# The first four chunks of q and k loaded in float32 by another queue, and the constants behind them

## The chip, the cores and the metric

The kernel runs on one core of a Trainium2 chip. A core has five engines with their own instruction streams: TensorE (PE in the profile, with its weight loads as PEld), VectorE (DVE), ScalarE (ACT), GpSimd (POOL) and SyncE (SP). Transfers between the chip's large memory and the core's on-chip memory run on 16 DMA engines that all queues share. Each engine that issues transfers has a queue of its own: GpSimd's is q0 in the profile, SyncE's q1, ScalarE's q10. The metric is the device time of one execution in microseconds.

## The reference

```python
qn = q / (np.linalg.norm(q, axis=1, keepdims=True) + 1e-06)
kn = k / (np.linalg.norm(k, axis=1, keepdims=True) + 1e-06)
s = kn.transpose(0, 2, 1) @ qn / tau
s = s - s.max(-1, keepdims=True)
a = np.exp(s)
a /= a.sum(-1, keepdims=True) + 1e-09
x = (v @ a).reshape(B * N, C)
logits = x @ w_gate
# softmax weights w of the two largest logits of each row, 0 elsewhere
out = x + sum over experts e of w[:, e] * ((x @ A[e]) @ B[e])
```

There are 4 batches of 6400 rows and 256 columns in float32. Within a batch, q and k give a 256x256 matrix (the Gram matrix of the columns, scaled by the column norms), its softmax `a` multiplies v, and each row of the result then goes through a mixture of 8 small adapters of rank 16. Read are 78.6 MB of q, k and v and 0.27 MB of constants; written are 26.2 MB.

## The kernel before

A batch's 6400 rows are split over the 128 partitions, 50 rows to a partition. One such set of 128 rows is a chunk, and 10 chunks are a tile: 640 KB of bfloat16 for each of q, k and v. Loads go through GpSimd's queue, which converts float32 to bfloat16 on the way. For the four batches there are 20 tiles of q and k together (four buffers) and 20 of v (five buffers).

The list `loads` (L89 to L97) fixes the order of all loads: first batch 0's five tiles of q and k (numbered 0 to 4 in this text), then batch 1's q and k mixed with batch 0's v, and so on. `load_more` (L107) issues the next entries of the list until a buffer is still in use by work not yet written into the program. GpSimd then waits for the release of the buffer and for one of eight DMA lanes, so that at most eight of its loads are under way. Tiles 0 to 3 fill the four buffers at once. Tile 4 (loaded in two parts, of 6 and 4 chunks) needs tile 0's buffer, batch 1's first tile needs tile 1's, and everything after it in the list stands behind it on GpSimd.

The program's order is written out by hand, instruction by instruction. At its start SyncE loads the three constants (L137 to L139): w_gate (8 KB, `wst`), moe_A (128 KB, `ast`, read in pieces of 128 bytes, 1024 of them) and moe_B (128 KB, `bst`, rows of 1 KB). GpSimd issues tiles 0 to 2 (L140), makes two identity matrices (L141 to L144) and issues tile 3 (L151). VectorE fills small constants and casts the three loaded ones to bfloat16 (L156 to L159); these casts stand ahead of all its other work and wait for the three transfers.

Then comes batch 0's loop over pairs of chunks (L479 to L486). For each pair, `square` squares q and k into one of five `sq` buffers (VectorE and ScalarE in turn), `gram` multiplies the two chunks of k by those of q on TensorE (L182), and `norm` sums the squares of the chunks four earlier by a matmul with ones (L194). When all 50 chunks are in, a chain of small steps (`chain0` to `chain6`) makes the softmax matrix and folds the cast constants into it; `ident_f` is first read in `chain1`, `ident` in `chain4`, `A_sb` and `wg_sb` in `chain5`.

After this the loop over slots mixes the work on batch 0's v (transposes L316, gating, L422 to L458, output copies L462) with the Gram matrix of the next batch, and so on through the batches. Outputs are collected in `ys`, eight buffers of 10 chunks, and sent by ScalarE's queue, late, and at the end by SyncE's.

Of the kernel before, what the change touches and what calls it, by code (L numbers as in the profile page):

```python
# [8 lines left out]
FP32 = mybir.dt.float32  # L9
BF16 = mybir.dt.bfloat16  # L10
# [6 lines left out]
def kernel(  # L17
# [16 lines left out]
    nc = tc.nc  # L34
    B, N, C = q.shape
    P = 128
    NC = N // P
    CC = C // P
    E = moe_w_gate.shape[1]
    R = moe_A.shape[2]  # L40
# [4 lines left out]
    PC = 10  # L45
    NPAIR = NC // 2
    NPT = B * NPAIR
    GRP = 5
    QKB, VB, YB = 4, 5, 8
    DEFER = 6  # L50

    GRAM = {1: (0, 20), 2: (24, 45), 3: (49, 67)}
# [2 lines left out]
    q_v = q.rearrange("b (p c) d -> b p c d", p=P)  # L55
    k_v = k.rearrange("b (p c) d -> b p c d", p=P)
# [3 lines left out]
    const = ctx.enter_context(tc.tile_pool(name="const", bufs=1))  # L60
# [4 lines left out]
    y_pool = ctx.enter_context(tc.tile_pool(name="yp", bufs=YB))  # L65
# [15 lines left out]
    for b, (first, last) in GRAM.items():  # L81
        n = last - first + 1
        for c in range(NC):
            s = first + c * n // NC
# [3 lines left out]

    loads = []  # L89
    for s in range(NC // PC):  # L90
        loads.append((-10 + s, "qk", 0, s, [PC] if s < NC // PC - 1 else [6, 4]))
        for b in range(1, B):
            loads.append((qk_need[b, s], "qk", b, s, [PC]))
        for b in range(B):
            loads.append((NPAIR * b + s * PC // 2 + 1, "v", b, s,
                          [6, 4] if b == B - 1 and s == NC // PC - 1 else [PC]))
    loads.sort(key=lambda x: x[0])  # L97
    tiles = {"qk": {}, "v": {}}
# [8 lines left out]
    def load_more(limit=1000):  # L107

        while limit and at_load[0] < len(loads):
            _, kind, b, s, parts = loads[at_load[0]]  # L110
            n = len(left[kind])
            if n >= bufs[kind] and left[kind][n - bufs[kind]]:
                return
            where[kind, b, s] = n
            left[kind].append(PC)
            c0 = s * PC
            if kind == "qk":
                t = qk_pool.tile([P, 2, PC, C], BF16, tag="qk", name="qk")
            else:
                t = v_pool.tile([P, PC, C], BF16, tag="v", name="vt")  # L120
            tiles[kind][b, s] = t
            o = 0
            for m in parts:
                if kind == "qk":
                    nc.gpsimd.dma_start(t[:, 0, o:o + m, :], q_v[b, :, c0 + o:c0 + o + m, :])  # L125
                    nc.gpsimd.dma_start(t[:, 1, o:o + m, :], k_v[b, :, c0 + o:c0 + o + m, :])
                else:
                    nc.gpsimd.dma_start(t[:, o:o + m, :], v_v[b, :, c0 + o:c0 + o + m, :])  # L128
                o += m
            at_load[0] += 1  # L130
            limit -= 1


    wst = const.tile([P, CC * E], FP32)
    ast = const.tile([P, E, CC * R], FP32)
    bst = const.tile([P, C], FP32)
    nc.sync.dma_start(wst, moe_w_gate.rearrange("(p cc) e -> p (cc e)", p=P))  # L137
    nc.sync.dma_start(ast, moe_A.rearrange("e (p cc) r -> p e (cc r)", p=P))
    nc.sync.dma_start(bst, moe_B.rearrange("e r d -> (e r) d"))  # L139
    load_more(3)  # L140
    ident = const.tile([P, P], BF16)  # L141
    make_identity(nc, ident)
    ident_f = const.tile([P, P], FP32)
    make_identity(nc, ident_f)  # L144
    ones_bf = const.tile([P, 2], BF16)
    nc.vector.memset(ones_bf, 1.0)
    ones_f = const.tile([P, P], FP32)
    nc.vector.memset(ones_f, 1.0)
    neg_inv_tau = const.tile([P, 1], FP32)
    nc.vector.memset(neg_inv_tau, -inv_tau)  # L150
    load_more(3)  # L151

    wg_sb = const.tile([P, CC, E], BF16)
    A_sb = const.tile([P, CC, E, R], BF16)
    ball_sb = const.tile([P, C], BF16)
    nc.vector.tensor_copy(wg_sb.rearrange("p cc e -> p (cc e)"), wst)  # L156
    for cc in range(CC):
        nc.vector.tensor_copy(A_sb[:, cc, :, :], ast[:, :, cc * R:(cc + 1) * R])
    nc.vector.tensor_copy(ball_sb, bst)  # L159


    acc, nrm, sqs = {}, {}, {}
# [1 line left out]
    def square(b, c, eng):  # L164

        s, o = divmod(c, PC)
        t = tiles["qk"][b, s]
        sq = sq_pool.tile([P, 2, 2, C], BF16, tag="sq", name="sq")
        sqs[b, c] = sq
        src = t[:, :, o:o + 2, :]  # L170
        if eng == "act":
            nc.scalar.activation(sq, src, ACT.Square)  # L172
        else:
            nc.vector.tensor_tensor(out=sq, in0=src, in1=src, op=OP.mult)  # L174

    def gram(b, c):
        if c == 0:
            acc[b] = ps_acc.tile([P, CC, C], FP32, tag="acc", name="acc")
        s, o = divmod(c, PC)
        t = tiles["qk"][b, s]  # L180
        for ic in range(CC):
            nc.tensor.matmul(  # L182
                acc[b][:, ic, :], t[:, 1, o, ic * P:(ic + 1) * P], t[:, 0, o, :],
                start=(c == 0 and ic == 0), stop=(c == NC - 1), skip_group_check=True)
        used("qk", b, c, 1)

    def norm(b, c):
        if c == 0:
            nrm[b] = ps_nrm.tile([P, 512], FP32, tag="nrm", name="nrm")
        sq = sqs[b, c - c % 2]  # L190
        for w in range(2):
            for ic in range(CC):
                j = w * CC + ic
                nc.tensor.matmul(  # L194
                    nrm[b][:, j:j + 1], sq[:, w, c % 2, ic * P:(ic + 1) * P], ones_bf[:, 0:1],
                    start=(c == 0 and j == 0), stop=(c == NC - 1), skip_group_check=True)
# [272 lines left out]
    def send(keep):  # L469


        eng = nc.scalar if keep else nc.sync
        while len(unsent) > keep:
            gr = unsent.pop(0)
            c0, n = 2 * (gr["f"] - gr["b"] * NPAIR), 2 * gr["n"]
            eng.dma_start(out_v[gr["b"], :, c0:c0 + n, :], gr["ys"][:, 0:n, :])


    for c in range(0, NC, 2):  # L479
        square(0, c, "act" if (c // 2) % 2 else "dve")  # L480
        gram(0, c)
        gram(0, c + 1)
        load_more()
        if c >= 4:
            norm(0, c - 4)
            norm(0, c - 3)  # L486
# [31 lines left out]
    while nz < NPT or zq is not None or dq is not None:  # L518
# [26 lines left out]
        dq, zq = zq, u  # L545
        send(max(0, min(DEFER, DEFER - (slot - GRAM[B - 1][1]) // 4)))
        if behind:
# [53 lines left out]
```

## Time and profile before

| | us |
|---|---|
| Median of three runs (257.8 to 257.87) | 257.8 |
| The profiled execution | 257.84 |
| Its span in the profile | 256.1 |
| Busy in the span: TensorE | 217.3 (85%) |
| ScalarE | 174.7 (68%) |
| VectorE | 150.6 (59%) |
| GpSimd | 34.5 (13%) |
| GpSimd's queue q0 (39.33 MB written), share of 16 engines | 75.7% |
| ScalarE's queue q10 (19.66 MB) | 18.6% |
| SyncE's queue q1 (6.82 MB) | 6.8% |

How to read the profile: the span is cut into 40 slices of 6.4 us, and each digit of a slice line is a busy share in tenths. The chain of waits follows the work that ended last back to its start; its lines give a start, a length and what ran. A wait is named by the engine that waited and by what released it. The queue lines give packets, megabytes and the time that the packets took as a share of 16 engines; since packets overlap, it can exceed 100%. GpSimd's queue is counted by what it writes, in bfloat16, while it reads twice as much. The times of a transfer run from its issue to its landing.

The first instructions around the change, by the timeline: SyncE issues w_gate at 0.74, moe_A at 1.18 and moe_B at 1.65 us. GpSimd issues tile 0 at 1.24 and 1.89 us, tiles 1 and 2 until 4.55 us, makes the identities between 4.49 and 5.63 us and issues tile 3 at 5.58 and 6.12 us. VectorE casts w_gate at 2.36, moe_A at 4.06 and moe_B at 10.03 us. Tile 0 lands at about 10.9 us, and TensorE's first matmul starts at 10.98 us.

### The profile page before, as it was taken

To read this page: it belongs to the slowest core of one execution; us is meant where nothing else is said; L and a number is where in the kernel's file an instruction comes from. 1 tells how busy PE (TensorE), PEld (TensorE's weight loads), DVE (VectorE), ACT (ScalarE), POOL (GpSimd) and SP (SyncE) were. 2 spreads that over 40 slices of the span, in tenths; PEclk is the share of its full clock that TensorE was granted. 3 is DMA by queue.
4 is the path that set the end of the run, shared out by engine and by line. 5 is a ranking of instruction groups with operands and counts; after the bars stand their busy time and mean duration, and the time that the engine had idled before them with its cause. 6 is when DMAs were issued, how large, how long until landed. Compare 5 with 4: busy or idle time off the path is not lost.

```text
span 256.1 us, 7681 instructions
## 1 busy us (share of the span) xinstructions
PE 217.3 (85%) x3256; PEld 192.1 (75%) x3256; DVE 150.6 (59%) x573; ACT 174.7 (68%) x288; POOL 34.5 (13%) x71
## 2 busy tenths in 40 slices
PE   0277694977898999999999999999799999999970
PEld 0256582766797978989999788988698789999960
DVE  1323234246746678676776776757477777777830
ACT  2234257366596698887977878787678768877870
POOL 8031131111112110120210203000000100000000
PEclk9987787579999999999999999999999999999997
DMA  6999999999999999999999999999999999999994
GB/s 117 222 214 214 210 215 215 214 213 215 214 215 214 215 214 216 213 215 214 213 215 215 313 281 248 246 285 300 229 281 271 325 337 366 421 418 425 425 380 181
DMA packets 13890, 66.30 MB, mean 259 GB/s; under 512 B 2592, under 2 KB 2720, under 8 KB 11424
## 3 DMA queue, kind: packets, MB, share of 16 engines
q0 software_dynamic: 9072, 39.33, 75.7%
q10 hardware_dynamic: 2160, 19.66, 18.6%
q1 hardware_dynamic: 2624, 6.82, 6.8%
q8 instruction: 25, 0.41, 0.6%
q14 instruction: 9, 0.07, 0.1%
HBM read 78.91 MB, written 26.21 MB: 411 GB/s over the span
## 4 chain that ended last, share of the span: by engine, by line
PE 44%; DMA 39%; DVE 8%; ACT 3%; issue 2%; POOL 1%; DVEq 0%; ACTq 0%; POOLq 0%
DMA qk<-in_k_dram 24%; PE y_ps L438 12%; DMA vt<-in_v_dram 8%; PE acc L182 7%; DMA qk<-in_q_dram 6%; PE zg L422 6%; PE y_ps L458 5%; PE vT_ps L316 5%; PE zg L446 3%; PE vT_ps L337 3%; PE nrm L194 2%; DVE gz L426 2%; ACT sq L172 2%; ACT ys L462 1%; DVE e L368 1%
## 5 line engine op out<-in xcount | busy, mean ns | idle before, releaser
L172 ACT ACTIVATE sq<-qk 128x1024 bf16<-128x1024 bf16 x87 | 89.0, 1053 | 36.4 <-DMA qk<-in_k_dram 35.3
L182 PE MATMUL acc<-qk 128*128 128x256 bf16 x400 | 78.3, 300 | 21.6 <-DMA qk<-in_k_dram 21.6
L462 ACT COPY ys<-y_ps 128x512 f32<-128x512 f32 x100 | 58.7, 587 | 18.0 <-PE y_ps L458 16.5
L438 PE MATMUL y_ps<-a_bf,vT 128*128 128x256 bf16 x400 | 59.9, 272 | 0.0
L182 PEld LDWEIGHTS <-qk 128*128 128x128 bf16 x400 | 33.7, 104 | 26.0 <-DMA qk<-in_k_dram 22.8
L194 PEld LDWEIGHTS <-sq 128*128 128x128 bf16 x800 | 46.2, 100 | 9.3 <-ACT sq L172 3.1
L426 DVE TENSOR_TENSOR gz<-zg,gate 128x256 bf16<-128x256 f32 x100 | 41.7, 417 | 14.6 <-PE zg L422 13.1
L194 PE MATMUL nrm<-ones_bf,sq 128*128 128x1 bf16 x800 | 44.9, 165 | 1.2 <-ACT sq L172 1.2
L327 DVE COPY vT<-vT_ps 128x512 bf16<-128x512 bf16 x63 | 26.7, 423 | 31.7 <-PE vT_ps L316 31.0
L316 PE MATMUL vT_ps<-ident,vt 128*128 128x128 bf16 x400 | 39.8, 224 | 2.0 <-DMA vt<-in_v_dram 1.8
L422 PE MATMUL zg<-wa_sb,vT 128*128 128x128 bf16 x400 | 38.3, 218 | 1.6 <-DVE gzT L452 1.4
L458 PE MATMUL y_ps<-ball_sb,gzT 128*128 128x256 bf16 x200 | 38.2, 273 | 0.0
L438 PEld LDWEIGHTS <-vT 128*128 128x128 bf16 x400 | 33.4, 97 | 2.5
L316 PEld LDWEIGHTS <-vt 128*128 128x128 bf16 x400 | 30.0, 99 | 5.4 <-DMA vt<-in_v_dram 2.9
L325 ACT COPY vT<-vT_ps 128x512 bf16<-128x512 bf16 x37 | 21.7, 586 | 10.6 <-PE vT_ps L316 9.0
L422 PEld LDWEIGHTS <-vT 128*128 128x128 bf16 x400 | 26.0, 96 | 3.8 <-issue 2.6
L446 PE MATMUL zg<-ident,gz 128*128 128x128 bf16 x200 | 27.6, 219 | 1.1 <-DVE gz L426 0.6
L452 DVE COPY gzT<-zg 128x256 bf16<-128x256 bf16 x90 | 25.3, 281 | 0.0
L125 POOL DMA_DIRECT2D qk<-in_q_dram x21 | 11.3, 540 | 83.0 <-ACT sq L172 18.6
L128 POOL DMA_DIRECT2D vt<-in_v_dram x21 | 11.1, 531 | 69.5 <-PE y_ps L458 39.2
L174 DVE TENSOR_TENSOR sq<-qk 128x1024 bf16<-128x1024 bf16 x13 | 8.7, 690 | 18.1 <-DMA qk<-in_k_dram 16.8
L446 PEld LDWEIGHTS <-gz 128*128 128x128 bf16 x200 | 15.1, 98 | 2.9 <-DVE gz L426 2.5
(54 smaller groups left out, 158.5 us busy)
## 6 DMA issues: line engine op xcount, KB each, us to landing
out_dram<-ys ACTq DMA_DIRECT2D x15, 1280.0 KB, 14.0
qk<-in_q_dram POOLq DMA_DIRECT2D x19, 640.0 KB, 22.1
qk<-in_k_dram POOLq DMA_DIRECT2D x19, 640.0 KB, 24.2
vt<-in_v_dram POOLq DMA_DIRECT2D x19, 640.0 KB, 24.5
out_dram<-ys SPq DMA_DIRECT2D x4, 1280.0 KB, 10.3
out_dram<-ys SPq DMA_DIRECT2D x5, 256.0 KB, 6.8
qk<-in_q_dram POOLq DMA_DIRECT2D x1, 384.0 KB, 16.4
qk<-in_k_dram POOLq DMA_DIRECT2D x1, 384.0 KB, 17.7
```

The lines of the kernel that those rows point to most:

```text
L172: nc.scalar.activation(sq, src, ACT.Square)
L182: nc.tensor.matmul(acc[b][:, ic, :], t[:, 1, o, ic * P:(ic + 1) * P], t[:, 0, o, :], start=(c == 0 and ic == 0), stop=(c == NC - 1), skip_ ...
L194: nc.tensor.matmul(nrm[b][:, j:j + 1], sq[:, w, c % 2, ic * P:(ic + 1) * P], ones_bf[:, 0:1], start=(c == 0 and j == 0), stop=(c == NC - 1 ...
L316: nc.tensor.matmul(pt[:, ic, sc * P:(sc + 1) * P], vt[:, o + sc, ic * P:(ic + 1) * P], ident, is_transpose=True, start=(i == 0), stop=(i = ...
L327: nc.vector.tensor_copy(dst, src)
L422: nc.tensor.matmul(z[:, sc, :], r["vT"][:, ic, sc, :], st[b]["wa"][:, ic, E:E + ER], start=(sc == 0 and ic == 0), stop=(sc == 1 and ic == ...
L426: nc.vector.tensor_tensor(out=gz.rearrange("p c (e r) -> p c e r", e=E), in0=z.rearrange("p c (e r) -> p c e r", e=E), in1=gr["gate"][:, r ...
L438: nc.tensor.matmul(y[:, sc, :], r["vT"][:, ic, sc, :], st[b]["a"][:, ic, :], start=(sc == 0 and ic == 0), stop=False, skip_group_check=True)
L446: nc.tensor.matmul(gt[:, sc, :], r["gz"][:, sc, :], ident, is_transpose=True, start=(sc == 0), stop=(sc == 1))
L452: nc.vector.tensor_copy(gzT, gt)
L458: nc.tensor.matmul(r["y"][:, sc, :], r["gzT"][:, sc, :], ball_sb, start=False, stop=(sc == 1), skip_group_check=True)
L462: nc.scalar.copy(gr["ys"][:, r["w"]:r["w"] + 2, :], r["y"])
```

## The change

Four chunks of q and four of k of batch 0 no longer go through GpSimd's queue. SyncE loads them first of all, in float32, into a buffer of the output pool (`stage`), 512 KB each. VectorE casts the four chunks of q to bfloat16 in two instructions, ScalarE those of k in two, into their places in tile 0; GpSimd's loads of tile 0 now begin at chunk 4. SyncE loads the constants behind the stage, moe_A last instead of moe_B. GpSimd issues tile 3 ahead of the two identities. The casts of the constants move into batch 0's loop, ahead of the work of chunk 14; VectorE meets them after its square of chunk 12 and ahead of its square of chunk 16.

```diff
+    FIRST = 4
...
-        loads.append((-10 + s, "qk", 0, s, [PC] if s < NC // PC - 1 else [6, 4]))
+        loads.append((-10 + s, "qk", 0, s, {0: [PC - FIRST], NC // PC - 1: [6, 4]}.get(s, [PC])))
...
+            o = PC - sum(parts)
...
-            o = 0
...
+    stage = y_pool.tile([P, 2 * GRP, C], FP32, tag="ys", name="stage")[:, 0:2 * FIRST, :].rearrange(
+        "p (w c) d -> p w c d", w=2)
+    nc.sync.dma_start(stage[:, 0, :, :], q_v[0, :, 0:FIRST, :])
+    nc.sync.dma_start(stage[:, 1, :, :], k_v[0, :, 0:FIRST, :])
...
     nc.sync.dma_start(wst, moe_w_gate.rearrange("(p cc) e -> p (cc e)", p=P))
+    nc.sync.dma_start(bst, moe_B.rearrange("e r d -> (e r) d"))
     nc.sync.dma_start(ast, moe_A.rearrange("e (p cc) r -> p e (cc r)", p=P))
-    nc.sync.dma_start(bst, moe_B.rearrange("e r d -> (e r) d"))
     load_more(3)
-    ident = const.tile([P, P], BF16)
-    make_identity(nc, ident)
-    ident_f = const.tile([P, P], FP32)
-    make_identity(nc, ident_f)
...
+    for c in range(0, FIRST, 2):
+        t = tiles["qk"][0, 0]
+        nc.vector.tensor_copy(t[:, 0, c:c + 2, :], stage[:, 0, c:c + 2, :])
+        nc.scalar.copy(t[:, 1, c:c + 2, :], stage[:, 1, c:c + 2, :])
+    load_more(1)
+    ident = const.tile([P, P], BF16)
+    make_identity(nc, ident)
+    ident_f = const.tile([P, P], FP32)
+    make_identity(nc, ident_f)
     load_more(3)
...
-    nc.vector.tensor_copy(wg_sb.rearrange("p cc e -> p (cc e)"), wst)
-    for cc in range(CC):
-        nc.vector.tensor_copy(A_sb[:, cc, :, :], ast[:, :, cc * R:(cc + 1) * R])
-    nc.vector.tensor_copy(ball_sb, bst)
+
+    def cast_constants():
+        nc.vector.tensor_copy(wg_sb.rearrange("p cc e -> p (cc e)"), wst)
+        for cc in range(CC):
+            nc.vector.tensor_copy(A_sb[:, cc, :, :], ast[:, :, cc * R:(cc + 1) * R])
+        nc.vector.tensor_copy(ball_sb, bst)
...
     for c in range(0, NC, 2):
+        if c == 14:
+            cast_constants()
         square(0, c, "act" if (c // 2) % 2 else "dve")
```

## The prediction

> **What bounds the kernel now.** I read the slices of the page first, then the chain of waits of the first 60 us, then the DMA queues in short windows.
>
> ```profile
> DMA  6999999999999999999999999999999999999994
> ```
>
> ```profile
> 0.64 0.60 issue
> 1.24 0.66 POOL qk L125
> 1.89 9.04 DMA qk<-in_k_dram
> ...
> 15.59 16.38 DMA qk<-in_q_dram
> ...
> 34.07 20.61 DMA vt<-in_v_dram
> 54.68 0.28 issue
> 54.97 24.46 DMA qk<-in_k_dram
> ```
>
> The DMA engines are full from the second slice almost to the end, and up to 79.4 us the chain is transfers. After that TensorE and the queue take turns: TensorE carries the chain from 80 to 154 us, a k load issued at 154.61 lands at 182.8, and the rest is TensorE. So the stream of transfers has no hole except at its start, and a stream that starts earlier moves all behind it. How much is lost there is told by the queues in 0 to 12 us and 12 to 24 us (packets, MB, share):
>
> ```profile
> q0 software_dynamic: 368, 1.72, 74.3%
> q1 hardware_dynamic: 1328, 0.27, 11.6%
> ```
>
> ```profile
> q0 software_dynamic: 565, 2.57, 104.8%
> ```
>
> A full GpSimd queue (q0) writes 2.57/12 = 0.214 MB/us. In the first 12 us it wrote 1.72 MB, which is 8.03 us of a full stream: 3.97 us are lost, to idleness and to the 0.27 MB of constants on SyncE's queue (q1).
>
> When each queue starts is seen in windows of 0.2 us: in 1.6 to 1.8 us
>
> ```profile
> q1 hardware_dynamic: 41, 0.00, 11.6%
> ```
>
> and the first packets of q0 only in 2.8 to 3.0 us:
>
> ```profile
> q1 hardware_dynamic: 257, 0.03, 103.3%
> q0 software_dynamic: 3, 0.02, 91.2%
> ```
>
> SyncE issued its first load at 0.74, GpSimd at 1.24 us: from issue to data 0.95 us on the one, 1.56 us on the other.
>
> **The change, part by part.**
>
> *The start.* SyncE's first issue, at 0.74 us, now carries 512 KB of q instead of 8 KB of w_gate, and k follows some 0.4 us later (its issues now take 0.38 to 0.57 us). So full traffic begins at 1.7 us, not at 2.8. The stage's 1.05 MB of float32 replace 0.52 MB of bfloat16 on q0. That is no extra work: at 0.214 MB/us the 0.52 MB cost 2.45 us, and in 222 to 234 us, where only float32 output moves, 426 GB/s make 1.05 MB cost 2.46 us. The stage keeps the engines busy until q0 starts at 2.8 us.
>
> The new loss is 1.7 us of idleness plus the constants, which no longer fall into an idle time. By bytes these cost 0.27/0.426 = 0.63 us. By q1's share of 0 to 4, 4 to 8 and 8 to 12 us (22.8%, 8.0%, 4.1% of 4 us) they cost 1.40 us. Between the two: moe_A's 1024 packets ran at 579 in 0.4 us (2.4 to 2.8 us), so 0.71 us, and the other 0.14 MB cost 0.33 us; I take 1.04. New loss 2.74 us (2.33 to 3.10), gain 3.97 - 2.74 = 1.2 us (0.9 to 1.6).
>
> The Trainium skill (DMA: Bandwidth & Descriptors, Specifications) gives a first-byte latency of about 1 us for the GpSimd path and 0.6 us for SyncE's. By it the start moves by the 0.5 us between the issues and 0.4 us of latency, 0.9 in all, an estimate that would give 256.9; the rows show 1.1, and I go by them.
>
> *The casts.* Two VectorE casts of 128x512 from float32. No row has them; the 128x256 cast (L159) took 0.29 us, the 128x512 bf16 copy 0.42 us, so 0.29 to 0.58 each; I take 0.5, 1.0 us in all. Two ScalarE copies: the 128x512 copy of L462 takes 0.59, 1.2 us in all. Both engines are idle until 11.02 us now, waiting for tile 0. The stage lands between about 5 us (ahead of q0) and 8 us (alternating with q0 row by row), the casts end by 9.5 us at the latest, and tile 0's six other chunks land at about 10.93 - 1.2 = 9.7. Cost nothing. Were this cover gone, tile 0 would be released later, which matters only if its successor's load (15.59 us) came after the queued three tiles (18 us of work) had run out.
>
> *GpSimd's order.* Tile 3's two loads come before the identities, so they are issued about 1.1 us earlier, behind a full queue: nothing gained. The identities come 1.1 us later; their first readers are at 39.46 and 41.99 us. Nothing.
>
> *Pool and lanes.* The stage takes the first of the eight output buffers, and each output still waits for the buffer and the DMA lane of eight before. Outputs first go out at 137.9 us. Nothing.
>
> *The casts of the constants.* 0.17 + 0.54 + 0.29 = 1.0 us of VectorE move from its idle start to behind its fourth square (c = 12, about 16 us). What queues behind is VectorE's square of c = 16 (at 18.26 us now), which TensorE reads (norm) only after tile 2 has landed, at 23.2 us, and which holds the release of tile 1; GpSimd issues into that buffer at 22.18 us. So up to about 21 us the cover is there, if the constants have landed. They are now issued last: this is where the change can turn (first rival).
>
> *Sum.* 257.84 us (the profiled run: span 256.1 and 1.7 around it; the median is 257.8) - 1.2 = 256.6. It is carried to the end because TensorE itself waits for transfers, 3.2 us in 36 to 62 us, 1.6 us in 62 to 90 us, and last for the k load that lands at 182.8 us; it starts earlier with them.
>
> **Rivals.**
>
> *Slower: moe_A is starved.* Where q1 and q0 both have work, they take turns packet by packet. In 5.8 to 9.0 us (moe_B's 1 KB rows against 5 KB rows) and in 142 to 147 us (10 KB output rows):
>
> ```profile
> q0 software_dynamic: 131, 0.59, 90.0%
> q1 hardware_dynamic: 125, 0.13, 13.9%
> ```
>
> ```profile
> q10 hardware_dynamic: 108, 1.11, 54.0%
> q0 software_dynamic: 105, 0.49, 47.4%
> ```
>
> moe_A is 64 packets of 128 B per engine, and a semaphore. Before, it ran at 2.2 to 3.7 us, mostly ahead of q0. Now k, w_gate, moe_B and moe_A (9 + 9 + 9 + 65 = 92 packets per engine) stand against q0, which has 9 per load: 18 of tile 0, 54 of tiles 1 to 3, then tile 4's. One for one, moe_A lands with the 20th of tile 4: 2.74 (lost) + 2.45 (stage) + 3.67 (rest of tile 0) + 3 x 6.12 (1.31 MB a tile) = 27.2 us to the end of tile 3, and 3.9 more, 31.1. VectorE stands still from 16 to 31 us with the square of c = 16 behind it. Tile 1 is released at 31.1 + 0.54 + 0.29 + 0.69 = 32.6, GpSimd's next load gives data 1.56 us later at 34.2, but the queue ran dry at 33.3 (five tiles of 6.12, and 2.74). That is 0.9 us idle, or up to 2.9 if the slowest engine counts (tile 4 lands at 36.45 us now, 2 us after its mean). TensorE also finishes batch 0 some 8 us late. Its later waits for DMA (3.2 us in 36 to 62, 1.6 in 62 to 90) and its low clock there (0.50 to 0.72 from 42 to 60 us) give back 5 to 8, so 0 to 3 us remain. In all 256.6 + 0.9 to 5.9: 257.5 to 262.5, middle 259.4. It decides when moe_A lands later than about 29.5 us. Against it: nothing in this trace shows small packets beside a full q0, and if a row's eight pieces go as one packet, the four need 36 turns, moe_A lands with the end of tile 1 near 15 us (2.74 + 2.45 + 3.67 + 6.12), and VectorE does not wait.
>
> The Trainium skill (DMA: Bandwidth & Descriptors, Queues, rings and completion order) says that an engine changes rows only after a whole packet, typically 9 to 17 descriptors. By that rule moe_A would need 4 to 7 turns and the forecast of 256.6 would hold; the two rows above show turns of one row each, so the rule does not settle it.
>
> *No change: swallowed.* TensorE's clock is granted at 0.50 to 0.94 between 12 and 60 us, in a pattern that follows its pauses. It now starts some 3 to 5 us earlier and pauses again for the rest of tile 0. TensorE is busy 28.4 us in 36 to 72 us; 4% more at a worse pattern is 1.2 us. Against it: in that stretch it waits for DMA anyway. Time 257.8.
>
> **Numbers.** Forecast 0.48 (256.2 to 256.9 by the bounds of the gain), starved moe_A 0.36, swallowed 0.12, 0.04 for a loss I don't see. A measurement of this kernel can tell 0.2%, 0.5 us. Faster: 0.48 and 0.02 of the starved case. Within 0.2%: 0.06 of the starved case, 0.09 of the swallowed one. Slower: 0.28, 0.03 and 0.04. The range goes from 256.1 (0.1 below the largest gain, about the spread of the runs) to 260.2 and leaves out the upper part of the starved case.
>
> **What would show it.** Right: first large packets on q1 at 1.7 us, q0's bytes in 0 to 12 us plus half of the stage's 1.05 MB near 1.98 MB (1.72 + 1.2 x 0.214), tile 1's first square near 15.9 us instead of 17.15, the k landing at 182.8 us about 1.2 us earlier, no long wait of VectorE for moe_A. Wrong: a VectorE wait on moe_A that ends near 30 us, a square of c = 16 behind it, GpSimd's fifth pair of q and k loads after 30 us, and a dip in the DMA row near 34 us.

## The result, and the profile after

The changed kernel takes 258.34 us (median of 13 runs), the kernel before 257.8 us in the same session: a ratio of 1.0021, 95% interval 1.0014 to 1.0029. It is 0.5 us slower, just at the edge of what can be told from no change. The forecast of 256.6 us has the wrong sign. What happened is the first rival, moe_A starved, in the lower part of its 257.5 to 262.5 us. One run of the kernel before and one with the stage of half the size took 493 us; no ratio below counts them.

The profiled execution of the changed kernel took 258.57 us with a span of 256.8. From its timeline (start, length, engine, line, what; in brackets the idle time before and what ended it):

```profile
16.82 0.17 DVE L169 CAST wg_sb<-wst 128x16 bf16<-128x16 f32 x1
...
32.07 0.36 DVE L171 CAST A_sb<-ast 128x128 bf16<-128x128 f32 x2 [15.08 <-DMA ast<-in_moe_A_dram]
32.34 0.29 DVE L172 CAST ball_sb<-bst 128x256 bf16<-128x256 f32 x1
32.55 1.89 DVE L187 TENSOR_TENSOR sq<-qk 128x1024 bf16<-128x1024 bf16 x3
...
33.86 0.53 POOL L126 DMA_DIRECT2D qk<-in_q_dram  x1 [16.95 <-DVE sq L187]
```

VectorE has cast w_gate and stands for 15.08 us until moe_A lands. Behind it in program order is the square of c = 16, which still reads tile 1, and GpSimd cannot load batch 1's first q into tile 1's buffer until it is done, at 33.86 us. Before, that issue stood at

```profile
22.18 0.53 POOL L125 DMA_DIRECT2D qk<-in_q_dram  x1 [4.32 <-PE nrm L194]
```

Why moe_A is late is seen in the issues of the first 12 us (size, us to landing) and in the queues from 12 to 24 us (packets, MB, share), both of the changed kernel:

```profile
stage<-in_q_dram SPq DMA_DIRECT2D x1, 512.0 KB, 3.7
stage<-in_k_dram SPq DMA_DIRECT2D x1, 512.0 KB, 4.5
...
bst<-in_moe_B_dram SPq DMA_DIRECT2D x1, 128.0 KB, 8.6
ast<-in_moe_A_dram SPq DMA_DIRECT2D x1, 128.0 KB, 29.5
```

```profile
q0 software_dynamic: 557, 2.52, 102.6%
q1 hardware_dynamic: 557, 0.07, 7.3%
```

557 packets against 557: for each row of up to 5 KB on GpSimd's queue (q0), SyncE's queue (q1) gets one piece of 128 bytes. The counts stay level in windows of 0.2 us as well: from 10.0 us on they are 8 and 8, 8 and 8, 8 and 9, 8 and 7, so the turns are of single packets and not of groups. The first of these windows, and moe_A's load in the kernel before:

```profile
q0 software_dynamic: 8, 0.04, 99.5%
q1 hardware_dynamic: 8, 0.00, 5.9%
```

```profile
ast<-in_moe_A_dram SPq DMA_DIRECT2D x1, 128.0 KB, 2.9
```

The same 128 KB that landed in 2.9 us before take 29.5 us.

What it costs is in the DMA row from 34 to 37 us (40 slices of 0.075 us), first the kernel before, then the changed one with what it moved:

```profile
DMA  8929294949999899998999969999699693996939
```

```profile
DMA  7463401010101099990958900099070993639939
GB/s 137 82 109 55 82 0 27 0 27 0 27 0 27 0 164 341 164 137 0 137 68 68 273 0 0 0 273 273 0 68 0 205 341 68 137 68 273 410 68 205
```

q0 has run dry for about a microsecond and then starts slowly. In 33 to 37 us the queues moved 0.53 MB where the kernel before moved 0.88: at 0.214 MB/us that is 1.6 us of the stream. The kernel does not win this back, as the chain of waits shows: the k load whose landing releases TensorE last starts 1.2 us later, though the stream began about a microsecond earlier. Before, and changed:

```profile
154.61 28.23 DMA qk<-in_k_dram
```

```profile
155.83 28.43 DMA qk<-in_k_dram
```

### The profile page after: what moved, and what is told of

Its sections match the earlier page's. It is cut to its first block, busy times and chain, and to the rows that moved or that the text cites. A ratio compares the mean times of both kernels' runs of the same rounds, so it can differ in the third digit from the quotient of the medians.

```text
span 256.8 us, 7690 instructions
## 1 busy us (share of the span) xinstructions
PE 217.2 (85%) x3256; PEld 191.8 (75%) x3256; DVE 150.8 (59%) x575; ACT 176.4 (69%) x290; POOL 35.1 (14%) x71
## 4 chain that ended last, share of the span: by engine, by line
PE 51%; DMA 31%; DVE 9%; ACT 4%; issue 2%; SPq 1%; POOL 0%; DVEq 0%; ACTq 0%
DMA qk<-in_k_dram 20%; PE y_ps L451 12%; DMA ast<-in_moe_A_dram 11%; PE acc L195 10%; PE zg L435 6%; PE vT_ps L329 6%; PE y_ps L471 5%; PE nrm L207 4%; PE zg L459 3%; PE vT_ps L350 3%; ACT sq L185 2%; DVE gz L439 2%; ACT ys L475 1%; PE nrm L241 1%; DVE e L381 1%
## 5 line engine op out<-in xcount | busy, mean ns | idle before, releaser
L475 ACT COPY ys<-y_ps 128x512 f32<-128x512 f32 x100 | 58.7, 587 | 19.1 <-PE y_ps L471 17.6
L439 DVE TENSOR_TENSOR gz<-zg,gate 128x256 bf16<-128x256 f32 x100 | 41.6, 417 | 15.2 <-PE zg L435 13.7
L459 PEld LDWEIGHTS <-gz 128*128 128x128 bf16 x200 | 15.1, 98 | 3.2 <-DVE gz L439 2.9
```

The costliest lines, as they stand in the source:

```text
L439: nc.vector.tensor_tensor(out=gz.rearrange("p c (e r) -> p c e r", e=E), in0=z.rearrange("p c (e r) -> p c e r", e=E), in1=gr["gate"][:, r ...
L459: nc.tensor.matmul(gt[:, sc, :], r["gz"][:, sc, :], ident, is_transpose=True, start=(sc == 0), stop=(sc == 1))
L475: nc.scalar.copy(gr["ys"][:, r["w"]:r["w"] + 2, :], r["y"])
```

## The experiments

Theory S: the earlier start is worth something, and the whole loss is VectorE's wait for a starved moe_A. Rival P: the early stage itself hurts. Within S, two prices were open: the queue that runs dry, and TensorE being late with batch 0. All times below are to be held against 257.8 to 258.0 us for the kernel before, run beside them; ratios are the ones to compare.

### Late casts

```diff
-        if c == 14:
-            cast_constants()
...
+    cast_constants()
     for c in range(NC - 4, NC):
         norm(0, c)
```

> The changed kernel with the casts of the constants moved behind batch 0's loop (ahead of its chain). Theory S (starved moe_A): the start is worth 1.0 us and all the loss is VectorE's wait for moe_A; moe_A still lands near 32 us, but nothing stands behind it, tile 1 is released near 18 us, the queue has no dip at 34 us: 256.8 us. Rival P (the early stage itself hurts, by TensorE's clock or a stage that ramps up slowly): no gain from this edit, about 258.3.

Measured: 257.29 us, ratio 0.9975 (0.9965 to 0.9985); a second time, beside another kernel, 257.33 us, 0.9979 (0.9970 to 0.9988). moe_A lands 29.8 us after its issue, as late as ever, but nothing waits for it. The changed kernel's loss becomes a gain of 0.2 to 0.25%, 0.5 to 0.6 us. Rival P falls: the stage is the same, and only the place of the casts differs. The gain is smaller than the 1.0 us expected; the section on the reasons says where the rest is.

### Casts ahead of chunk 24

```diff
-        if c == 14:
+        if c == 24:
```

> The changed kernel with the casts ahead of chunk 24 instead of chunk 14. VectorE still waits for moe_A, from about 23 to 32 us, and TensorE stands still with it, but tile 1 is released near 18 us. If the cost of the wait is the queue that runs dry (1.7 us at 34 to 36 us in the changed kernel): the dip is gone and the time is that of the late casts, about 256.8 to 257.0. If the cost is TensorE being late with batch 0: most of it stays, 257.8 to 258.3.

Measured: 257.24 us, ratio 0.9972 (0.9963 to 0.9981), the same as the late casts. This run parts the two prices. Its timeline and its waits of TensorE:

```profile
21.96 0.53 POOL L126 DMA_DIRECT2D qk<-in_q_dram  x1 [5.06 <-PE nrm L207]
...
32.00 0.36 DVE L171 CAST A_sb<-ast 128x128 bf16<-128x128 f32 x2 [8.79 <-DMA ast<-in_moe_A_dram]
```

```profile
PE nrm L207 <- DVE sq L187: 6.3, 1, 6.3
```

VectorE still stands for 8.79 us and TensorE for 6.3 us. But tile 1 was released before the wait, the three loads that GpSimd makes next were issued from 21.96 us, and the DMA row from 34 to 37 us has no hole:

```profile
DMA  5999959499693999939999399993999969969699
```

TensorE is late with batch 0 all the same: the batch's chain begins at 42.9 us here, at 38.9 with the late casts and at 45.2 in the changed kernel. So 4.0 us of TensorE's lateness cost nothing that can be measured, and the dry queue is the price; the last 2.3 us of the changed kernel's lateness no run tries by themselves.

### moe_A in rows of 1 KB

```diff
-    nc.sync.dma_start(ast, moe_A.rearrange("e (p cc) r -> p e (cc r)", p=P))
+    nc.sync.dma_start(ast.rearrange("p e x -> p (e x)"), moe_A.rearrange("e (u w) r -> (e u) (w r)", w=16))
```

> The changed kernel with moe_A's 128 KB loaded as 128 rows of 1 KB, 8 packets per engine instead of 64 (rows and columns of A end up in other places than the calculation needs, so that its values are others; the work is the same). Theory S with turns by packet: moe_A has 9 turns, lands near 12 us, VectorE does not wait: 256.8 to 257.0. If turns go by bytes and not by packets, moe_A lands as late as before and the time stays at 258.3.

Measured: 257.05 us, ratio 0.9969 (0.9958 to 0.9979). The same bytes stand in the same place of the order, but in an eighth of the packets. (This kernel leaves A's elements in other places than the calculation needs, so its output is not the reference's; the work is the same.)

```profile
ast<-in_moe_A_dram SPq DMA_DIRECT2D x1, 128.0 KB, 11.7
```

11.7 us instead of 29.5, so turns go by packets and not by bytes, and VectorE's cast starts at 17.3 us behind its square without a wait. The number of pieces is the cause of the starving.

### moe_A loaded twice

```diff
-    stage = y_pool.tile([P, 2 * GRP, C], FP32, tag="ys", name="stage")[:, 0:2 * FIRST, :].rearrange(
-        "p (w c) d -> p w c d", w=2)
+    whole = y_pool.tile([P, 2 * GRP, C], FP32, tag="ys", name="stage")
+    stage = whole[:, 0:2 * FIRST, :].rearrange("p (w c) d -> p w c d", w=2)
...
+    nc.sync.dma_start(whole[:, 2 * FIRST, :].rearrange("p (e x) -> p e x", e=E),
+                      moe_A.rearrange("e (p cc) r -> p e (cc r)", p=P))
     nc.sync.dma_start(ast, moe_A.rearrange("e (p cc) r -> p e (cc r)", p=P))
```

> The changed kernel with moe_A loaded twice, first into a free part of the stage's buffer, where it is not read: 65 more packets per engine ahead of the moe_A that VectorE waits for. Theory S: it lands only when q0 has run dry, near 35 us instead of 32; the dip at 34 us is 3 us longer, 261 to 262 us. If the price of the changed kernel does not come from this wait: 258.3 to 258.6, by 0.3 us of bytes.

Measured: 262.26 us, ratio 1.0171 (1.0157 to 1.0185). The longer wait costs more, a little beyond the 261 to 262 us expected:

```profile
36.39 0.36 DVE L173 CAST A_sb<-ast 128x128 bf16<-128x128 f32 x2 [19.33 <-DMA ast<-in_moe_A_dram]
...
38.18 0.53 POOL L126 DMA_DIRECT2D qk<-in_q_dram  x1 [21.20 <-DVE sq L189]
```

GpSimd's issue is 4.32 us later than in the changed kernel (38.18 against 33.86), and the time grows by 3.9 us, of which up to 0.3 us may be the second copy's own bytes: once the queue is dry, further delay is paid nearly one for one.

### moe_A last in the kernel before

Only these two parts of the change, without the stage:

```diff
     nc.sync.dma_start(wst, moe_w_gate.rearrange("(p cc) e -> p (cc e)", p=P))
+    nc.sync.dma_start(bst, moe_B.rearrange("e r d -> (e r) d"))
     nc.sync.dma_start(ast, moe_A.rearrange("e (p cc) r -> p e (cc r)", p=P))
-    nc.sync.dma_start(bst, moe_B.rearrange("e r d -> (e r) d"))
...
     for c in range(0, NC, 2):
+        if c == 14:
+            cast_constants()
```

> The kernel before, without the stage, with only two parts of the change: moe_A issued last of the constants and the casts ahead of chunk 14. Theory S: moe_A is issued at 1.65 us and meets q0's rows, as moe_B did before (first data at 5.8 us); 65 turns of about 0.39 us put it near 31 us. VectorE waits from about 18 us, the queue runs dry near 35 us for 1 to 2 us: 258.8 to 259.8. If moe_A still gets through ahead of q0, as it did in the kernel before: no wait, 257.8.

Measured: 257.79 us, ratio 0.9997 (0.9988 to 1.0006), no change. The time is that of the second expectation, but not by its path, and the first is missed. moe_A is starved here too, but VectorE gets it 3.2 us earlier than in the changed kernel:

```profile
28.89 0.36 DVE L159 CAST A_sb<-ast 128x128 bf16<-128x128 f32 x2 [11.48 <-DMA ast<-in_moe_A_dram]
...
30.68 0.54 POOL L125 DMA_DIRECT2D qk<-in_q_dram  x1 [12.84 <-DVE sq L175]
```

A wait of 11.48 us on VectorE costs nothing that can be measured, because GpSimd's next load comes at 30.68 us, while q0 still has rows. The DMA row from 34 to 37 us has no hole:

```profile
DMA  8989899999998999969696896966969669696696
```

This order brings q0 forward by very little (6.86 MB by 36 us against 6.83 before, 0.14 us), so not much of a cost can hide behind a gain. The order of the constants alone was harmless. It took the stage ahead of them. w_gate and moe_B land here at about 2.4 and 3.7 us; in the changed kernel, behind the stage, they land at about 8.1 and 10.7 us, and their 18 packets per engine take turns with q0 ahead of moe_A's. q0's rows run out at nearly the same time in both: of tiles 0 to 4 the changed kernel has written its 6.02 MB by 34.4 us, this one its 6.55 MB by 34.6 us. So it is moe_A's later landing that pushes the wait over the edge. Together with the runs above: issued at 30.68 us the load is in time, at 33.86 us it costs 1.1 us against the late casts, at 38.18 us 5.0. If the delay is paid one for one, both of the last two put the edge near 33 us, 1.4 us before q0's last rows.

### Constants ahead of the stage

```diff
-    nc.sync.dma_start(stage[:, 0, :, :], q_v[0, :, 0:FIRST, :])
-    nc.sync.dma_start(stage[:, 1, :, :], k_v[0, :, 0:FIRST, :])
...
     nc.sync.dma_start(wst, moe_w_gate.rearrange("(p cc) e -> p (cc e)", p=P))
-    nc.sync.dma_start(bst, moe_B.rearrange("e r d -> (e r) d"))
     nc.sync.dma_start(ast, moe_A.rearrange("e (p cc) r -> p e (cc r)", p=P))
+    nc.sync.dma_start(bst, moe_B.rearrange("e r d -> (e r) d"))
+    nc.sync.dma_start(stage[:, 0, :, :], q_v[0, :, 0:FIRST, :])
+    nc.sync.dma_start(stage[:, 1, :, :], k_v[0, :, 0:FIRST, :])
```

> The changed kernel with the constants issued ahead of the stage, in the order of the kernel before. Theory S: moe_A lands near 4 us, no wait; the stage comes some 1.4 us later on SyncE, full traffic near 2.8 us, part of the gain of the start is lost: 257.0 to 257.5. Rival P: 258.3, since the stage is still there.

Measured: 258.17 us, ratio 1.0008 (0.9999 to 1.0016): moe_A is early and VectorE does not wait for it, yet the gain is gone. The 257.0 to 257.5 us of theory S were missed, and the time is near rival P's 258.3. But the late casts have the same stage and gain, so the stage does not hurt by itself; here it has lost its early place. Now the stage is what meets q0:

```profile
stage<-in_q_dram SPq DMA_DIRECT2D x1, 512.0 KB, 8.6
stage<-in_k_dram SPq DMA_DIRECT2D x1, 512.0 KB, 12.5
```

The traffic up to 4 us is no more than that of the kernel before (76 and 100 GB/s in 3.2 to 4.0 us, 99 and 143 before), and tile 0 is complete only at 15.2 us. What SyncE issues first gets the free time ahead of q0, and the rest of its queue meets q0's rows.

### k's stage on ScalarE's queue

```diff
     ctx.enter_context(tc.manual_schedule())
...
+    nc.sync.dma_start(stage[:, 0, :, :], q_v[0, :, 0:FIRST, :])
+    nc.scalar.dma_start(stage[:, 1, :, :], k_v[0, :, 0:FIRST, :])
     nc.scalar.preload_act_table_set("natural_log_exp_and_others")
...
-    nc.sync.dma_start(stage[:, 0, :, :], q_v[0, :, 0:FIRST, :])
-    nc.sync.dma_start(stage[:, 1, :, :], k_v[0, :, 0:FIRST, :])
```

with the late casts.

> The kernel with the late casts (after the loop), and k's stage issued by ScalarE ahead of its table load, so that both halves of the stage are issued at 0.74 us. The stage alone moved only 80 to 270 GB/s between 1.6 and 2.8 us. If that ramp is k's later issue (1.18 us), the stream is fuller by 0.2 to 0.4 us and the time is 0.2 to 0.4 us below the late casts: 256.8 to 257.0. If the first packets of a queue are slow whoever issues them, no difference: 257.2.

Measured: 257.26 us, ratio 0.9971 (0.9961 to 0.9981): no difference from the late casts. 113, 92 and 205 GB/s moved in the three windows of 0.4 us from 1.6 us, against 133, 82 and 113 with one queue. ScalarE issued k's stage at 0.74 us, but its first data came only after 2.4 us; until then q's rows ran alone, and no faster than with one queue. So issuing k earlier does not fill the slow first microsecond. What makes it slow stays open.

### A stage of half the size

```diff
-    FIRST = 4
+    FIRST = 2
```

with the late casts.

> The kernel with the late casts and a stage of two chunks of q and of k instead of four. If the gain is that of the early start alone (1.7 against 2.8 us, and q0's slow first packets covered), half the stage gives the same: 257.1 to 257.4. If it goes with the bytes moved off q0, half the gain is left: 257.5 to 257.6.

Measured: 257.48 us, ratio 0.9982 (0.9972 to 0.9992). It lies between the two expectations, and its interval overlaps that of the late casts: whether the gain grows with the stage is not settled.

### moe_A on ScalarE's queue

```diff
     ctx.enter_context(tc.manual_schedule())
...
+    nc.scalar.dma_start(ast, moe_A.rearrange("e (p cc) r -> p e (cc r)", p=P))
     nc.scalar.preload_act_table_set("natural_log_exp_and_others")
...
-    nc.sync.dma_start(ast, moe_A.rearrange("e (p cc) r -> p e (cc r)", p=P))
```

with the casts ahead of chunk 14, as in the change.

> The changed kernel, casts ahead of chunk 14 as in the change, with moe_A issued by ScalarE ahead of its table load, at 0.74 us beside the stage, instead of last by SyncE. Theory S: its 64 packets take turns with the 16 rows of the stage and are done before q0's rows come (about 4.8 us), or soon behind them, VectorE does not wait: 257.0 to 257.4, like the late casts. If three queues starve it too, it lands beyond 20 us; below 29 us that costs nothing (as in the run with moe_A last and no stage), beyond 31 us it costs 1 us or more. Should the small packets slow the stage down in the first 4 us, the gain shrinks: 257.5 to 257.8.

> The kernel with the late casts once more, beside the one above on the same chip, so that the two can be compared: 257.1 to 257.4 by theory S.

Measured: 257.33 us, ratio 0.9977 (0.9968 to 0.9986); the late casts beside it 257.33 us, 0.9979. moe_A lands 4.5 us after its issue at 0.75 us, ahead of q0's rows, and VectorE's cast at 17.6 us does not wait:

```profile
ast<-in_moe_A_dram ACTq DMA_DIRECT2D x1, 128.0 KB, 4.5
```

The casts stand where the change put them, so their place alone does not cost; the late load does. Two ways out of the starving, a later reader and an earlier load, give the same time, and both beat the kernel before by about 0.2%.

## Why the prediction was wrong

**What bounds the kernel: right.** The stream of transfers has no hole but at its start, so a hole made elsewhere is paid nearly in full (moe_A twice: 4.32 us later, 3.9 us longer), and compute that stops beside a full queue costs nothing that can be measured (VectorE 11.48 us, TensorE 6.3 us). One reading was loose, without bearing on the sum: the chain is not transfers throughout up to 79.4 us, since from 10.98 to 15.25 us TensorE carries it.

**The casts of the constants: the step that failed.** It read "up to about 21 us the cover is there, if the constants have landed". They had not. The working of the first rival was right almost line by line: one turn per packet, moe_A near 31.1 us (32.0), tile 1's release at 32.6 (33.2), the dry queue at 33.3 (the DMA row falls from 34 us). I gave it 0.36 because no row showed pieces of 128 bytes beside a full q0 and a row's eight pieces might go as one packet. But both rows that I had, with 1 KB and 10 KB packets, showed a turn for a packet whatever its size; they should have weighed more than a grouping that no row showed. The Trainium skill (DMA: Bandwidth & Descriptors, Queues, rings and completion order) lets an engine drain a packet of typically 9 to 17 descriptors from one queue before it changes to another. The trace does not agree for these pieces: beside q0's rows they went one each, in windows of 0.2 us too. The prediction also took this rule to speak for its forecast, which it does not: q0 would drain as many of its rows in each of its turns. An estimate by that page gives 4 turns of 17 rows or 7 of 9, which is 63 to 68 rows of q0 ahead of moe_A's end, as many as one for one.

**The price of that rival: too high in its middle.** Of its terms, 0.9 to 2.9 us of idle queue came to 1.6 (0.35 MB missing in 33 to 37 us). The 0 to 3 us for TensorE's lateness came to nothing that can be measured, by the casts ahead of chunk 24. In all the wait cost 1.1 us against the late casts. The rival had charged TensorE for a stretch in which it waits for transfers anyway.

**The gain of the start: the right mechanism, half the size.** Forecast 1.2 us, measured 0.5 to 0.7 us in the four kernels that do not pay for moe_A (late casts, measured twice, chunk 24, two queues, moe_A on ScalarE), and 0.8 with moe_A in rows. The term that was mis-sized is "full traffic begins at 1.7 us". It begins, but not full. The late casts in 1.6 to 2.8 us:

```profile
DMA packets 32, 0.13 MB, mean 109 GB/s; under 512 B 0, under 2 KB 0, under 8 KB 32
```

Against the 426 GB/s that I counted, 109 GB/s for 1.2 us lose 0.9 us, and the rest up to 4.8 us another 0.2. In bytes, q0 by 36 us with the late casts, and in the kernel before:

```profile
q0 software_dynamic: 1798, 6.39, 88.2%
```

```profile
q0 software_dynamic: 1780, 6.83, 95.4%
```

With 0.52 MB for the stage, 36 - 6.91/0.214 = 3.7 us are lost, 1.0 more than the 2.74 of the sum, and the slow first packets are large enough to account for it. The kernel before has lost 36 - 6.83/0.214 = 4.1 us by then, so 0.4 us of gain are left in the stream, near the time measured. Half or more of what the early start brought went into its own slow first packets. Why they are slow no run shows; an earlier issue of k did not help.

**Swallowed: no.** What is gained at the start (0.4 us in the stream) does arrive at the end once no dry queue eats it. TensorE's pattern in the first 60 us differs in all these runs without a trace in the time.

**The parts costed at nothing held.** The casts of the stage ran at 4.42 to 5.32 us (VectorE, 0.43 and 0.56 us each) and 5.70 to 6.84 us (ScalarE, 0.62), all before tile 0's remaining chunks at 9.9 us. The identities and the output pool left no wait; GpSimd's wait of 1.17 us for a landing, ahead of its issue at 16.37 us, stood beside a full queue.

## What to carry to other kernels

Where transfers bound a kernel, ask of every engine that is made to wait not how long it stands, but which load is issued behind it and whether the queue still has work at that moment: here 11.5 us of VectorE's waiting cost nothing, and 15.1 us, with the next load 3.2 us later, cost 1.1. When a small load is moved behind a saturated queue, count its packets, not its bytes, and compare them with the other queue's packets in the same time. A load's reader moves with the load: late load, late reader, as far as the first real use allows.

## What the runs showed that I had not expected

A piece of 128 bytes takes a whole turn beside a full queue: 128 KB in 1024 pieces took 29.5 us, in 128 rows 11.7 us, and ahead of the queue 2.9 us. The first packets of the stage run at about a quarter of the full rate for 1.2 us (109 of 426 GB/s), and at about a third with a second queue. And q0's first data came at about 4.8 us with the stage ahead of it (2.8 us before), though GpSimd issued at 1.23 and 1.24 us: nearly all of the stage's 16 rows per engine went first, so here a queue that was issued 0.5 us earlier kept the engines to itself for longer than that.
